# A retention layer with a cosine-gated MLP: another load order at the start, weights released earlier, and the planner's transfer times reset

## The chip, the core and the metric

The kernel runs on one core of one Trainium2 chip. Its engines are TensorE (PE: matmuls; the load of a matmul's stationary operand is shown apart as PEld), VectorE (DVE), ScalarE (ACT), GpSimd (POOL) and SyncE (SP), which here only issues transfers. Each engine runs its own instructions in the order in which they were written; semaphores hold an instruction until what it needs is there. Sixteen DMA engines move the data, fed by queues: `q1` (hardware) carries what SP issues, `q0` (software) what POOL issues. The metric is device microseconds of one execution.

## The reference

Q, K and V have 8 batches, 8 heads, 576 positions and 64 features. The scores are decayed by a power of a constant per head, with no softmax, and the result goes through two matrix products with h cos(h) between them:

```
scores = (q @ k.T) / sqrt(64)
ret    = (scores * gamma_h ** (pos_i - pos_j), zero above the diagonal) @ v     # per batch and head
x      = ret, heads side by side                                                # 4608 x 512
h      = x @ w_in                                                               # 512 -> 2048
out    = (h * cos(h)) @ w_out                                                   # 2048 -> 512, float32
```

The inputs and the output are float32 in memory; matmuls take bf16.

## The kernel before, in words

**Units and blocks.** A unit (b, g) is one batch's 256 positions (g = 0 or 1) or, for g = 2, the last 64 positions of four batches, with all heads. A block is two units: 512 tokens, and there are nine. The first four units in order are (0,0), (1,0), (0,1), (1,1): blocks 0 and 1. For each unit the kernel loads Q, K and V (`load`, L465, issued by SP), scales or casts them to bf16 (`unit`: `qnat`, `natk`, `natv`; the decay is split into a factor on Q and one on V, and `natv` is made by two POOL multiplies), transposes Q and K to `qt`, `kt` (on PE for blocks 0 and 1, `tpe`, L525; by DMA for the rest, `txb`, L540), multiplies K by Q (`scores`), masks on DVE (`pt`, L611), adds up a running state K^T V per batch (`st`, with copies `sba`, `sbb`, `sbr`), and forms the output from masked scores and state (`outputs`), which ACT copies from PSUM to `xt` (L461).

**The MLP.** `mlp1` (L762) multiplies one slice f of 128 hidden features by `win`, over half a block (256 columns) or all of it (512); ACT takes the sine of the result shifted by pi/2 (`cb`, L770) and DVE multiplies it back in (`gt`, L773). `wino2` (L867) is the second matmul in a form with seven products for eight; it needs sums of `gt` (`S`, L828 and L834) and of `wout` (`wsums`, L807), all on DVE. Before the change the blocks 0, 1 and 2 go through `mlp1` in halves, the others whole. Slices go in the order of FORDER: slab 0 of `win` (f 0 to 3), then slabs 2, 1 and 3. A slab of `win` or `wout` is a quarter of the matrix, loaded and cast by a transfer that POOL issues (L742, L746).

**The planner.** None of this order is written out. Each operation becomes a task with an engine, a duration in ns, its readers and writers and, for some, a due time (`prio`). `Graph.run` places tasks one by one at the time at which engine, operands and buffers would be free, by those durations, and the order of the placed tasks becomes the program. For a transfer it takes all transfers as one line: a duration `dma` behind the previous one, and then `tail` until the data may be used. A task with `port=True` is kept from running beside one of the other of DVE and POOL. PSUM has six banks `bk`; a PE task that takes more than two at once may be picked ahead of others to get them (the list `due`, L251). Where the plan leaves a gap on PE, `emit` puts in filler matmuls on a matrix of ones (`warm`, L409). So a changed duration in the planner changes no instruction, only the place of instructions in each engine's line.

**The start before.** SP issues K, Q, V of (0,0), then K, Q, V of (1,0). Slabs 0 and 2 of `win` wait for the K of (1,0), slabs 1 and 3 for its Q. The loads of (0,1) and (1,1) wait for slab 2, the slabs of `wout` for the Q of (1,1), and the loads of (2,0) for slab 2 of `wout`.

Of the kernel before, what the change touches and what calls it, by code (L numbers as in the profile page):

```python
# [11 lines left out]
B, H, S, D = 8, 8, 576, 64  # L12
# [117 lines left out]
class Graph:  # L130


    BACKLOG = 2500
    AHEAD, FETCH = 2000, 6500

    def __init__(self, pools):
        self.tasks, self.wr, self.rd = [], {}, {}
# [70 lines left out]
    def run(self, dma_rate):  # L208
        self.prios()
        free = {e: 0.0 for e in ("pe", "act", "dve", "pool", "sp")}  # L210
# [3 lines left out]
        est, order = {}, []  # L214
# [19 lines left out]
        def pick(e):  # L234
            cand = []
            for t in ready[e]:
                a = slots(t)
                if a is None:
                    continue
                s = max(free[e], est[t], a)  # L240
                if e == "pe" and t.count:
                    k = (seen + t.count - 443) // 256
                    if k >= 0 and 443 + 256 * k > seen and k in asked:
                        s = max(s, asked[k] + self.FETCH - t.dur * (443 + 256 * k - seen) / t.count)
                if t.port:
                    s = max(s, port_free["pool" if e == "dve" else "dve"])
                if t.dma is not None and e != "pool":
                    s = max(s, dma_free - self.BACKLOG)
                cand.append((s, t))
            if e == "pe":  # L250
                due = [t for t in ready[e] if all(any(f is not None and f <= free[e] + 1500 for f in self.pools[b.pool])  # L251
                                                  for b in t.allocs if b.pool != "bk") and self.first(t) and sum(b.pool == "bk" for b in t.allocs) > 2 and est[t] <= free[e] + 1500]
# [12 lines left out]

        n = 0
        while n < len(self.tasks):
# [9 lines left out]
            s, t = best  # L277
            e = t.eng
# [14 lines left out]
            for b in t.allocs:  # L293
                pool = self.pools[b.pool]
# [28 lines left out]
class Kernel:  # L323
# [4 lines left out]
                sbb=(256, BF16), sbr=(256, BF16), xt=(2048, BF16), gt=(NF * TB, BF16), s=(1024, BF16),  # L328
                cb=(TB, BF16), os=(1024, F32), sn=(TB, F32))
    FORDER = [0, 1, 2, 3, 8, 9, 10, 11, 4, 5, 6, 7, 12, 13, 14, 15]  # L330
    SPLIT = 2
    NOXBAR = {0, 1}
    PERIOD, T0, T1 = 28800, 14000, 30000

# [124 lines left out]
    def copy(self, eng, dur, dst, src, r, w, **kw):  # L459
        if eng == "act":  # L460
            return self.one(eng, dur, lambda e: e.activation(dst(), src(), AF.Copy), r=r, w=w, **kw)  # L461
        return self.one(eng, dur, lambda e: e.tensor_copy(dst(), src()), r=r, w=w, port=True, **kw)  # L462


    def load(self, which, u, rows, gate):  # L465

        stg = self.staged[which, u] = Buf("stg" + which)
        src = self.src["qkv".index(which)]
        for i, (p0, n, o, ny, b, r0) in enumerate(rows):
            at, w = (b * H * S + r0) * D, ny * D  # L470
            self.one("sp", 500, lambda e, p0=p0, n=n, o=o, w=w, at=at: e.dma_start(  # L471
                ap(self.at(stg), 1024, p0, n, o, [w, H], [1, w]), bass.AP(src, at, [[w, n], [S * D, H], [1, w]])),
                r=gate, w=[(stg, i)], sem=lambda i=i: f"{which}{stg.slot}_{i}", dma=1830 if ny == 2 else 600, tail=720)
        return stg

    def unit(self, u, fast=False, gate=()):

        rem = u[1] == 2
        t = self.tiles[u] = {}
        for which, nat, dst in (("k", "natk", "kt"), ("q", "qnat", "qt"), ("v", "natv", None)):  # L480
            if rem:
                rows = [(64 * (b % 2), 64, 512 * (b // 2), 1, 4 * u[0] + b, 512) for b in range(4)]
            else:
                rows = [(0, 128, 0, 2, u[0], 256 * u[1])]
            stg = self.load(which, u, rows, gate)
            rs = [(stg, i) for i in range(len(rows))]
            nb = t[nat] = Buf(nat)
            for y in range(2):
                def out(y=y, nb=nb):
                    return ap(self.at(nb), 1024, 0, 128, 512 * y, [256, 2], [64, 4], [1, D])  # L490

                o, w = (512 * y, D) if rem else (D * y, 2 * D)
                hs = [[4, 2], [1, 4]] if which == "v" else [[1, 2], [2, 4]]

                def inp(stg=stg, o=o, hs=[[n * w, c] for n, c in hs]):
                    return ap(self.at(stg), 1024, 0, 128, o, *hs, [1, D])
                if which == "k":
                    eng = ("act", "pool")[y] if fast else "pool"
                    self.copy(eng, {"act": 520, "dve": 610, "pool": 560}[eng], out, inp, rs, [(nb, y)])
                else:  # L500
                    tab, key = (self.WV, "wv") if which == "v" else (self.WQ, "wq")
                    col = 32 if rem else 16 * u[1] + 8 * y
                    eng = "dve" if fast and which == "q" else "pool"
                    self.one(eng, 610 if eng == "dve" else 1000, lambda e, out=out, inp=inp, tab=tab, col=col, hs=hs: e.tensor_tensor(  # L504
                        out(), inp(), ap(tab, 40, 0, 128, col, *hs, [0, D]), ALU.mult),
                        r=rs + [(key,)], w=[(nb, y)], port=True)
# [29 lines left out]
    def txb(self, u):  # L536
        parts = []
        for i, (nat, dst) in enumerate((("natk", "kt"), ("qnat", "qt"))):
            src, dst = self.tiles[u][nat], self.tiles[u][dst]
            parts.append((1300 * (i + 1), lambda e, src=src, dst=dst: e.dma_start_transpose(  # L540
                ap(self.at(dst), 1024, 0, 128, 0, [128, 8], [1, 128]), ap(self.at(src), 1024, 0, 128, 0, [1, 1024])),
                [(src, y) for y in range(2)], [(dst, y) for y in range(2)],
                {"sem": lambda dst=dst: f"t{dst.pool}{dst.slot}"}))
        self.G.add("sp", 2600, parts, dma=4300)

    LANES = [(i, j) for i in range(2) for j in range(2)]

# [101 lines left out]
    def outputs(self, u, prio, late, join=None):  # L649
# [57 lines left out]
        def copies():  # L707
            for s in range(2):
# [3 lines left out]
                else:  # L712
                    dst = lambda s=s: ap(self.at(xt), 2048, 0, 128, 1024 * half + 128 * s, [256, 4], [1, 2], [2, 64])
                    src = lambda s=s: ap(self.at(ob[s]), 512, 0, 128, 0, [128, 4], [64, 2], [1, 64])
                self.copy("act", 590, dst, src, [(ob[s],)], [(xt, half, s)])

        if join is not None:
            join.append((main, cross, reads, writes, copies))
# [21 lines left out]
    def load_w(self, which, s, gate, prio):  # L740
# [4 lines left out]
        else:  # L745
# [64 lines left out]
    def wino2(self, j, base, span):  # L810

        gt = self.gt[j]
        S_ = {(i, q): Buf("s") for i in range(1, 5) for q in range(2)}

        def a(k, h, q):
            return ap(self.at(gt), NF * TB, 0, 128, (8 * k + 4 * q) * TB + 256 * h, [TB, 4], [1, 256])
# [7 lines left out]
        for q in range(2):  # L824
            for i, x, y, r, op in (
                    (1, lambda q=q: a(0, 1, q), lambda q=q: a(1, 1, q), ak(0, 1, q) + ak(1, 1, q), ALU.add),
                    (2, lambda q=q: sv(1, q), lambda q=q: a(0, 0, q), ak(0, 0, q) + [(S_[1, q],)], ALU.subtract)):
                self.one("dve", 610, lambda e, i=i, q=q, x=x, y=y, op=op: e.tensor_tensor(sv(i, q), x(), y(), op),  # L828
                         r=r, w=[(S_[i, q],)], port=True, name=f"S{i}_{j}")
        for q in range(2):  # L830
            for i, x, y, r, op in (
                    (3, lambda q=q: a(0, 0, q), lambda q=q: a(0, 1, q), ak(0, 0, q) + ak(0, 1, q), ALU.subtract),
                    (4, lambda q=q: a(1, 0, q), lambda q=q: sv(2, q), ak(1, 0, q) + [(S_[2, q],)], ALU.subtract)):
                self.one("dve", 610, lambda e, i=i, q=q, x=x, y=y, op=op: e.tensor_tensor(sv(i, q), x(), y(), op),  # L834
                         r=r, w=[(S_[i, q],)], port=True, name=f"S{i}_{j}")
# [71 lines left out]
    def graph(self):  # L907
# [46 lines left out]
        for x in range(4):  # L954
            self.load_w("wout", x, gate, 200 + x)
# [55 lines left out]
```

## Time and profile before

| | us |
|---|---|
| median of 3 runs | 303.77 (302.33 to 304.1) |
| the profiled execution | 302.27 |
| its span in the profile | 300.6 |
| PE busy | 284.7 (95%) |
| DVE busy | 224.1 (75%) |
| ACT busy | 169.2 (56%) |
| POOL busy | 104.2 (35%) |

The profile shows one execution. An engine's busy time is the time in which at least one of its instructions was running; a matmul is counted for about 0.27 us although the next follows after 0.11 us, so a busy PE is not always a PE at its full rate. "Idle before" names what ended a wait, by the semaphore that came last. The granted clock is the share of full speed that the throttle allowed PE.

### The profile page before, as it was taken

To read this page: it belongs to the slowest core of one execution; us is meant where nothing else is said; L and a number is where in the kernel's file an instruction comes from. 1 tells how busy PE (TensorE), PEld (TensorE's weight loads), DVE (VectorE), ACT (ScalarE), POOL (GpSimd) and SP (SyncE) were. 2 spreads that over 40 slices of the span, in tenths; PEclk is the share of its full clock that TensorE was granted. 3 is DMA by queue.
4 is the path that set the end of the run, shared out by engine and by line. 5 is a ranking of instruction groups with operands and counts; after the bars stand their busy time and mean duration, and the time that the engine had idled before them with its cause. 6 is when DMAs were issued, how large, how long until landed. Compare 5 with 4: busy or idle time off the path is not lost.

```text
span 300.6 us, 9042 instructions
## 1 busy us (share of the span) xinstructions
PE 284.7 (95%) x3785; PEld 202.8 (67%) x3785; DVE 224.1 (75%) x390; ACT 169.2 (56%) x315; POOL 104.2 (35%) x125
## 2 busy tenths in 40 slices
PE   7789799999898999999999999999999999999994
PEld 2457577788687876667676767666766676666683
DVE  3667998999994889697959595968687857666721
ACT  5468785468556565645564556465554574545420
POOL 3821970885749204826263515071100000000000
PEclk9999999999999999999999999999999999999999
DMA  7999799999999279996999995782103000300115
GB/s 202 252 206 287 185 180 233 258 240 315 252 274 227 63 186 285 217 226 203 184 301 199 262 218 115 175 218 65 37 1 142 2 2 2 140 0 2 71 72 140
DMA packets 101640, 49.87 MB, mean 166 GB/s; under 512 B 43488, under 2 KB 97248, under 8 KB 101600
## 3 DMA queue, kind: packets, MB, share of 16 engines
q1 hardware_dynamic: 97376, 45.10, 62.8%
q0 software_dynamic: 4224, 4.19, 8.7%
q8 instruction: 30, 0.49, 0.7%
q14 instruction: 10, 0.08, 0.1%
HBM read 36.70 MB, written 9.44 MB: 154 GB/s over the span
## 4 chain that ended last, share of the span: by engine, by line
PE 75%; DMA 13%; POOL 5%; ACT 2%; DVE 2%; issue 1%; SPq 0%; DVEq 0%
PE bk L762 35%; PE bk L867 33%; DMA stgq<-in_q_dram 7%; PE bk L571 6%; DMA wout<-in_moe_w_out_dram 4%; DMA win<-in_moe_w_in_dram 3%; POOL natv L504 2%; PE st L571 1%; POOL qnat L504 1%; ACT xt L461 1%; DVE gt L773 1%; ACT cb L770 0%; POOL wout L746 0%; DVE s L828 0%; SPq L471 0%
## 5 line engine op out<-in xcount | busy, mean ns | idle before, releaser
L770 ACT ACTIVATE cb<-bk,cpi 128x256 bf16<-128x256 f32 (+1 forms) x192 | 108.1, 584 | 82.5 <-PE bk L762 79.2
L762 PE MATMUL bk<-xt,win 128*128 128x256 bf16 (+1 forms) x768 | 143.2, 326 | 2.7 <-issue 1.5
L773 DVE TENSOR_TENSOR gt<-bk,cb 128x256 bf16<-128x256 f32 (+1 forms) x192 | 103.0, 553 | 50.1 <-ACT cb L770 46.5
L762 PEld LDWEIGHTS bk<-xt,win 128*128 128x128 bf16 x768 | 71.9, 98 | 40.6 <-issue 2.7
L504 POOL TENSOR_TENSOR natv<-stgv,wv 128x512 bf16<-128x512 f32 x36 | 40.0, 1134 | 34.6 <-PE bk L571 20.4
L611 DVE TENSOR_TENSOR pt<-bk,tr 128x512 bf16<-128x512 f32 x68 | 42.6, 679 | 2.8 <-PE bk L571 2.8
L504 POOL TENSOR_TENSOR qnat<-stgq,wq 128x512 bf16<-128x512 f32 x32 | 35.1, 1119 | 18.5 <-DMA stgq<-in_q_dram 18.5
L462 POOL CAST natk<-stgk 128x512 bf16<-128x512 f32 x34 | 21.9, 670 | 53.4 <-DMA stgk<-in_k_dram 40.9
L867 PE MATMUL bk<-wout,gt 128*128 128x256 bf16 x288 | 36.7, 273 | 2.4 <-DVE gt L773 1.5
L867 PE MATMUL bk<-tw,s 128*128 128x256 bf16 x288 | 36.9, 273 | 1.0 <-ACT xt L461 1.0
L867 PE MATMUL bk<-wout,s 128*128 128x256 bf16 x288 | 36.4, 273 | 0.0
L867 PEld LDWEIGHTS bk<-tw,s 128*128 128x128 bf16 x288 | 27.8, 98 | 9.7 <-ACT xt L461 1.2
L867 PEld LDWEIGHTS bk<-wout,gt 128*128 128x128 bf16 x288 | 27.6, 98 | 9.4 <-issue 1.8
L867 PEld LDWEIGHTS bk<-wout,s 128*128 128x128 bf16 x288 | 27.8, 98 | 6.5
L461 ACT ACTIVATE sn<-bk 128x512 f32<-128x512 f32 x27 | 16.1, 597 | 17.2 <-PE bk L867 17.2
L879 DVE TENSOR_TENSOR os<-bk,sn 128x512 f32<-128x512 f32 x27 | 18.4, 681 | 9.2 <-PE bk L867 9.2
L461 ACT ACTIVATE xt<-bk 128x512 bf16<-128x512 f32 x36 | 23.7, 728 | 0.5 <-PE bk L571 0.5
L867 PE MATMUL bk<-tw,gt 128*128 128x256 bf16 x144 | 18.5, 273 | 0.0
L867 PEld LDWEIGHTS bk<-tw,gt 128*128 128x128 bf16 x144 | 14.1, 98 | 4.2
L834 DVE TENSOR_TENSOR s<-gt 128x1024 bf16<-128x1024 bf16 x18 | 15.4, 858 | 0.2
L828 DVE TENSOR_TENSOR s<-gt 128x1024 bf16<-128x1024 bf16 x18 | 15.1, 836 | 0.5
L834 DVE TENSOR_TENSOR s<-gt,s 128x1024 bf16<-128x1024 bf16 x18 | 14.7, 815 | 0.2
(56 smaller groups left out, 166.9 us busy)
## 6 DMA issues: line engine op xcount, KB each, us to landing
stgk<-in_k_dram SPq DMA_DIRECT2D x16, 512.0 KB, 6.5
stgq<-in_q_dram SPq DMA_DIRECT2D x16, 512.0 KB, 7.1
stgv<-in_v_dram SPq DMA_DIRECT2D x16, 512.0 KB, 6.7
out_dram<-os SPq DMA_DIRECT2D x16, 512.0 KB, 3.2
win<-in_moe_w_in_dram POOLq DMA_DIRECT2D x4, 512.0 KB, 9.1
wout<-in_moe_w_out_dram POOLq DMA_DIRECT2D x4, 512.0 KB, 10.3
stgk<-in_k_dram SPq DMA_DIRECT2D x8, 128.0 KB, 3.5
stgq<-in_q_dram SPq DMA_DIRECT2D x8, 128.0 KB, 3.3
```

The costliest lines, as they stand in the source:

```text
L461: return self.one(eng, dur, lambda e: e.activation(dst(), src(), AF.Copy), r=r, w=w, **kw)
L462: return self.one(eng, dur, lambda e: e.tensor_copy(dst(), src()), r=r, w=w, port=True, **kw)
L504: self.one(eng, 610 if eng == "dve" else 1000, lambda e, out=out, inp=inp, tab=tab, col=col, hs=hs: e.tensor_tensor(out(), inp(), ap(tab, ...
L571: return lambda e: e.matmul(out(), lhs(), rhs(), start=start, stop=True, skip_group_check=True)
L611: self.one("dve", 610, lambda e, r=r, b=b, pt=pt: e.tensor_tensor(ap(self.at(pt), 1024, 0, 128, 512 * r, [64 * ny * ny, 8 // ny // ny], [1 ...
L762: inst = e.matmul(ap(self.at(bk), 512, 0, 128, 0, [1, n]), ap(self.WIN, 4 * DFF, 0, 128, c * DFF + 128 * f, [1, 128]), ap(self.at(xt), 204 ...
L770: self.one("act", 70 + n, lambda e: e.activation(ap(self.at(cb), TB, 0, 128, 0, [1, n]), ap(self.at(bk), 512, 0, 128, 0, [1, n]), AF.Sin, ...
L773: self.one("dve", 75 + n / 0.96, lambda e: e.tensor_tensor(ap(self.at(gt), NF * TB, 0, 128, f * TB + 256 * h0, [1, n]), ap(self.at(bk), 51 ...
L828: self.one("dve", 610, lambda e, i=i, q=q, x=x, y=y, op=op: e.tensor_tensor(sv(i, q), x(), y(), op), r=r, w=[(S_[i, q],)], port=True, name ...
L834: self.one("dve", 610, lambda e, i=i, q=q, x=x, y=y, op=op: e.tensor_tensor(sv(i, q), x(), y(), op), r=r, w=[(S_[i, q],)], port=True, name ...
L867: inst = e.matmul(ap(self.at(bank), 512, 0, 128, 256 * tt, [1, 256]), l(f, tt), rr(f), start=(first and f == 0 and tt == 0), stop=True, sk ...
L879: self.one("dve", 610, lambda e: e.tensor_tensor(view(h, c), ap(self.at(bank), 512, 0, 128, 0, [256, 2], [1, 256]), ap(self.at(sn[name]), ...
```

## The change

At the start (units built with `fast`) Q is loaded and prepared ahead of K. Slab 0 of `win` waits for the Q of unit (0,0), slab 2 for the Q of (1,0), slabs 1 and 3 for the K of (1,0). `mlp1` of block 0 goes in halves only for slabs 0 and 2, and whole for slabs 1 and 3; block 2 goes whole (SPLIT 1). For three units (SWIFT) one of the two copies to `xt` moves from ACT to DVE. The S sums of block 0 wait for slab 0 of `wout`. In the planner, the time to use of later loads goes from 720 to 1800 ns, the weights' from 2600 + 1500 to 2750 or 3000 + 1900, the DMA transposes' from 4300 to 3000, two POOL durations grow by 20 and 30 ns, DVE copies from PSUM and DVE's multiplies of Q no longer keep POOL away, and the scores of (0,1) may be picked ahead although they take two banks (DUE).

```diff
+    DUE = ("ses/0.1",)
...
-    ... sum(b.pool == "bk" for b in t.allocs) > 2 and est[t] <= free[e] + 1500]
+    ... sum(b.pool == "bk" for b in t.allocs) > 2 - (t.name in self.DUE) and est[t] <= free[e] + 1500]
...
-    SPLIT = 2
+    SPLIT = 1
+    HALVES = (0, 2)
+    SWIFT = ((0, 0), (1, 0), (0, 1))
...
-        return self.one(eng, dur, lambda e: e.tensor_copy(dst(), src()), r=r, w=w, port=True, **kw)
+        return self.one(eng, dur, lambda e: e.tensor_copy(dst(), src()), r=r, w=w, port=eng == "pool", **kw)
...
-                ..., dma=1830 if ny == 2 else 600, tail=720)
+                ..., dma=1840 if ny == 2 else 600, tail=720 if fast else 1800)
...
-        for which, nat, dst in (("k", "natk", "kt"), ("q", "qnat", "qt"), ("v", "natv", None)):
+        todo = [("k", "natk", "kt"), ("q", "qnat", "qt"), ("v", "natv", None)]
+        for which, nat, dst in [todo[i] for i in ((1, 0, 2) if fast else (0, 1, 2))]:
...
-        self.G.add("sp", 2600, parts, dma=4300)
+        self.G.add("sp", 2600, parts, dma=3000)
...
-                self.copy("act", 590, dst, src, [(ob[s],)], [(xt, half, s)])
+                self.copy("dve" if s and u in self.SWIFT else "act", 590, dst, src, [(ob[s],)], [(xt, half, s)])
...
-                 sem=f"{which}{s}", dma=2600, tail=1500, prio=prio)
+                 sem=f"{which}{s}", dma=2750 if which == "win" else 3000, tail=1900, prio=prio)
...
+        late = [("wout", 0, 0)] * (j == 0)
...
-                         r=r, w=[(S_[i, q],)], port=True, name=f"S{i}_{j}")
+                         r=r + late, w=[(S_[i, q],)], port=True, name=f"S{i}_{j}")
...
-        for x, which, pr in ((0, "k", 100), (2, "k", 101), (1, "q", 102), (3, "q", 103)):
-            self.load_w("win", x, [(st[which, (1, 0)], 0)], pr)
+        for x, which, pr in ((0, "q", 100), (2, "q", 101), (1, "k", 102), (3, "k", 103)):
+            self.load_w("win", x, [(st[which, (min(x, 1), 0)], 0)], pr)
...
-        for h in range(2):
-            for i, f in enumerate(self.FORDER):
-                self.mlp1(0, f, (h,), T0 + 435 * (2 * i + h))
+        for i, f in enumerate(self.FORDER):
+            for ses in ((0,), (1,)) if f // 4 in self.HALVES else ((0, 1),):
+                self.mlp1(0, f, ses, T0 + 435 * (2 * i + ses[0]))
```

More of the change, by code (lines that the diff above doesn't have):

```diff
@@ L251, in pick @@
                 due = [t for t in ready[e] if all(any(f is not None and f <= free[e] + 1500 for f in self.pools[b.pool])
-                                                  for b in t.allocs if b.pool != "bk") and self.first(t) and sum(b.pool == "bk" for b in t.allocs) > 2 and est[t] <= free[e] + 1500]
+                                                  for b in t.allocs if b.pool != "bk") and self.first(t) and sum(b.pool == "bk" for b in t.allocs) > 2 - (t.name in self.DUE) and est[t] <= free[e] + 1500]
                 due = [t for t in due if t.prio <= min(x.prio for x in ready[e]) + self.AHEAD]
@@ L461, in copy, with load @@
             return self.one(eng, dur, lambda e: e.activation(dst(), src(), AF.Copy), r=r, w=w, **kw)
-        return self.one(eng, dur, lambda e: e.tensor_copy(dst(), src()), r=r, w=w, port=True, **kw)
-    def load(self, which, u, rows, gate):
+        return self.one(eng, dur, lambda e: e.tensor_copy(dst(), src()), r=r, w=w, port=eng == "pool", **kw)
+    def load(self, which, u, rows, gate, fast):
         stg = self.staged[which, u] = Buf("stg" + which)
@@ L472, in load @@
                 ap(self.at(stg), 1024, p0, n, o, [w, H], [1, w]), bass.AP(src, at, [[w, n], [S * D, H], [1, w]])),
-                r=gate, w=[(stg, i)], sem=lambda i=i: f"{which}{stg.slot}_{i}", dma=1830 if ny == 2 else 600, tail=720)
+                r=gate, w=[(stg, i)], sem=lambda i=i: f"{which}{stg.slot}_{i}", dma=1840 if ny == 2 else 600, tail=720 if fast else 1800)
         return stg
@@ L484, in unit @@
                 rows = [(0, 128, 0, 2, u[0], 256 * u[1])]
-            stg = self.load(which, u, rows, gate)
+            stg = self.load(which, u, rows, gate, fast)
             rs = [(stg, i) for i in range(len(rows))]
@@ L498, in unit @@
                     eng = ("act", "pool")[y] if fast else "pool"
-                    self.copy(eng, {"act": 520, "dve": 610, "pool": 560}[eng], out, inp, rs, [(nb, y)])
+                    self.copy(eng, {"act": 520, "dve": 610, "pool": 580}[eng], out, inp, rs, [(nb, y)])
                 else:
@@ L503, in unit @@
                     eng = "dve" if fast and which == "q" else "pool"
-                    self.one(eng, 610 if eng == "dve" else 1000, lambda e, out=out, inp=inp, tab=tab, col=col, hs=hs: e.tensor_tensor(
+                    self.one(eng, 610 if eng == "dve" else 1030, lambda e, out=out, inp=inp, tab=tab, col=col, hs=hs: e.tensor_tensor(
                         out(), inp(), ap(tab, 40, 0, 128, col, *hs, [0, D]), ALU.mult),
-                        r=rs + [(key,)], w=[(nb, y)], port=True)
+                        r=rs + [(key,)], w=[(nb, y)], port=eng == "pool")
             if dst:
@@ L834, in wino2 @@
                 self.one("dve", 610, lambda e, i=i, q=q, x=x, y=y, op=op: e.tensor_tensor(sv(i, q), x(), y(), op),
-                         r=r, w=[(S_[i, q],)], port=True, name=f"S{i}_{j}")
+                         r=r + late, w=[(S_[i, q],)], port=True, name=f"S{i}_{j}")
         A, Bb, C = Buf("bk"), Buf("bk"), Buf("bk")
```

## The prediction

> **What bounds the kernel now.** I read the page's engine shares first, then the busy time by stage, then the PE timeline of the start and the DMA queues. Busy time by stage (columns: PE, PEld, DVE, ACT, POOL busy us with instruction counts, granted clock, DMA share, GB/s):
>
> ```profile
> 0.00:17.00 17.00, 12.93 (x192) 6.63 (x192) 8.51 (x28) 8.81 (x15) 10.63 (x25) 1.00 0.99 224
> 17.00:28.00 11.00, 9.70 (x143) 7.83 (x144) 7.53 (x19) 8.35 (x20) 0.46 (x1) 1.00 1.21 246
> 28.00:46.00 18.00, 14.95 (x233) 11.55 (x231) 17.39 (x32) 13.73 (x31) 14.27 (x16) 1.00 0.97 196
> 46.00:100.00 54.00, 50.99 (x830) 42.23 (x829) 46.45 (x88) 33.52 (x76) 33.22 (x34) 1.00 1.12 255
> 100.00:283.00 183.00, 182.73 (x2275) 122.87 (x2273) 139.26 (x220) 101.08 (x168) 45.66 (x50) 1.00 0.56 131
> ```
>
> From 100 to 283 us PE idles 0.27 us: nothing is to be won there. The tail (PE ends at 296.4, span 300.6) is the last product and its store, in the same order after the change. So only the first 100 us count. Steady rates: eight 256-wide matmuls take 0.87 us (0.109 each), eight 512-wide 1.73 (0.216), 32 attention matmuls 0.57, eight transposes 0.45. All the work at these rates is 384 x 0.109 + 384 x 0.216 + 1008 x 0.109 + 1920 x 0.0178 + 64 x 0.057 = 272.5 us; PE ends at 296.4, so 23.9 us are lost: 12.8 before 17.0 (only 4.2 us of work is done by then), some 2.2 to 26.8, 4.5 from there to 46, and 4.4 to 100. PE stretches at the start:
>
> ```profile
> 1.12 4.02 PE L409 MATMUL bk<-one 128*128 128x512 bf16 x9 [1.12 <-DVE lg L432]
> ...
> 9.45 0.64 PE L571 MATMUL bk<-qt,kt 64*64 64x128 bf16 x32
> ...
> 16.99 0.61 PE L762 MATMUL bk<-xt,win 128*128 128x256 bf16 x4 [0.17 <-DMA win<-in_moe_w_in_dram]
> ...
> 20.44 2.12 PE L762 MATMUL bk<-xt,win 128*128 128x256 bf16 x18 [1.28 <-issue]
> ...
> 45.70 1.05 PE L867 MATMUL bk<-wout,gt 128*128 128x256 bf16 x8 [0.83 <-DMA wout<-in_moe_w_out_dram]
> ```
>
> The first product waits for `win` slab 0 until 16.99. The 1.28 us at 20.44 stop in the middle of a group of four, where the program has no wait; the page calls it issue.
>
> **Q ahead of K, unit (0,0).** The same six loads in another order: Q lands where K did (about 5.0), K where Q did (6.8). Before, after Q at 6.81 came two DVE multiplies in series (1.29), a transpose, a copy, scores at 9.45. After, the multiplies are done by 6.4 while K flies; K's two casts run beside each other (ACT 0.63, POOL 0.61), then transpose 0.24, copy 0.60: scores at 8.7. The four mask multiplies (0.63 each) end at 11.7 instead of 13.54, since DVE no longer stops among them for the second Q (landed 12.2).
>
> **The first slab's release.** Slab 0 moves from behind unit (1,0)'s K to behind (0,0)'s Q, past two POOL instructions (K's cast and natv): its issue (3.17 us for four, so 0.8) falls into POOL's idle time until 5.06 and costs nothing there. Slab 2 now waits for (1,0)'s Q, slabs 1 and 3 for its K, 1.6 us ahead of (1,0)'s natv. Issue to landing was 5.6 us for slab 0, so 10.6 at the earliest. The price is paid by the loads that the slab now runs among. A slab moves in 2.6 us (11 us for four), a load in 1.8. What two queues do to each other is seen once, when the loads of unit (0,1) were issued at 20.54 against the last slab. From 22 to 23.5 the slabs' queue alone moved; from 24 to 26 both did:
>
> ```profile
> q0 software_dynamic: 305, 0.31, 124.2%
> ```
> ```profile
> q1 hardware_dynamic: 1255, 0.63, 108.7%
> q0 software_dynamic: 28, 0.02, 6.7%
> ```
>
> So bounds for V of (1,0), the last of the six: 16.7 if the slabs queue behind loads already issued (13.4 before plus a slab, plus the tail to landing), 24.6 if all slabs go first, as in the first of these windows. I take 18.6, packets sharing once both queues are fed, since the new loads are in flight before the slabs, unlike at 20.54; both ends stay in the range. [...]
>
> PE then: V of (0,0) lands between 8.9 and 11.1 (its natv starts at 8.76 now; the slab takes up to 2.4 from it), natv takes 2.08 on POOL, outputs end at 13 to 14.5; the transposes of (1,0)'s Q (landing 13.6) stand ahead of the first product, so it starts at 15.3 against 16.99. Sixteen matmuls (1.74), K's transposes and scores run to 18.2; natv of (1,0) is done at 18.6 + 2.08 + 0.3 = 21.0 and slab 2 lands at about 20.5 to 21, so PE stands some 2.5 us; then four products, outputs and 44 products end at 27.6 (26.8 at the near bound). Before, 58 of these 64 were done at 26.8. SP's next loads, those of (0,1), wait for slab 2 as they did (20.5), and move by no more than half a us. Gain 0 to 0.7, **I take 0.3**: the start mostly swaps a wait for the slab for a wait for V.
>
> **Half or full width.** Blocks 0 (half of it) and 2 go to 512 columns: 48 halves become 24 wholes. PE's columns are the same. The rows:
>
> ```profile
> L770 ACT ACTIVATE cb<-bk,cpi 128x512 bf16<-128x512 f32 x96 | 66.1, 689 | 64.2 <-PE bk L762 63.8
> L770 ACT ACTIVATE cb<-bk,cpi 128x256 bf16<-128x256 f32 x96 | 42.0, 480 | 18.3 <-PE bk L762 15.4 <-DVE gt L773 2.8
> ```
> ```profile
> L773 DVE TENSOR_TENSOR gt<-bk,cb 128x512 bf16<-128x512 f32 x96 | 65.5, 688 | 39.2 <-ACT cb L770 38.0 <-PE bk L867 0.5
> ...
> L773 DVE TENSOR_TENSOR gt<-bk,cb 128x256 bf16<-128x256 f32 x96 | 37.4, 419 | 10.9 <-ACT cb L770 8.5 <-PE bk L762 2.0
> ```
>
> ACT saves 48 x 0.480 - 24 x 0.689 = 6.5 us, DVE 48 x 0.419 - 24 x 0.688 = 3.6 and takes three `xt` copies from ACT. No row has that copy on DVE: between 0.42 (its bf16 copy of a bank) and 0.73 (ACT's own); I take 0.68, as its combine of a bank: 2.0. Net DVE -1.6 us, in the stages where it is busy 17.39 of 18 and 46.45 of 54 us.
>
> **The planner's times.** They cost no instruction; they move the order. Between 28 and 46 the sums of block 0 (S, L828/L834), which kept DVE busy then, go behind `wout` slab 0, and products of block 1 come ahead of block 0's second matmul. I walk the new PE order with the rows: after the 64 products, eight full ones, then transposes of (0,1) between full products to 33; scores; 0.5 us for K's cast of (1,1), since POOL works in series from 27 to 43 as before; 0.6 for the masks of (0,1); 40 half products, two `wout` groups: 46.2 with 2.0 us lost against 4.5, of which the 0.83 above is one. **2.5 us.** The added wait for `wout` slab 0 (landed at 41.1) stands on DVE ahead of (1,1)'s masks; DVE reaches it at 43.1, so 2 us of cover; beyond that each us is PE's. From 46 on DVE has 25 gt x 0.43, 8 S x 0.8, 5 tw and 2 wout x 0.7, 3 combines and 4 masks x 0.68 = 26.8 us of queue beside 23.8 us of PE work: PE waits about 2.5 to 3 against 4.4 before. **1.7 us.** Each walk could miss as much as it finds (0 for both) or leave half the losses still more (1 us each way).
>
> **Sum.** 0.3 + 2.5 + 1.7 = 4.5. A walk by hand finds only the waits it looks for; I take four fifths, 3.6 us. The profiled execution took 302.27 (span 300.6 and 1.7 around it), 1.5 under the median 303.77; the new runs may fall on either, so I set out from 303.0: **299.4**.
>
> **Rivals.**
> *Within 1%: nothing but the start's small gain (0 to 2 us, 301 to 303).* For it: DVE is full in 28 to 90 us and stays so; a stop removed on PE returns as a wait for DVE. Against: S moves out of 28 to 46, and ACT and DVE lose instructions. This also covers the case that the new planner times change the order but not the time.
> *Slower: V of (1,0) starves.* If three slabs run unshared from 16 to 24, V lands at 24.6, natv ends at 26.7, the 64 products at 33.0 instead of 27.6: 5.4 late. Later waits swallow 1 us; with the later gains kept the end is near 302, with half of them lost near 306. It decides from V landing past about 22. For it the 22 to 23.5 window, against it the 24 to 26 one.
> *The PE clock.* The nine 512-wide matmuls at 1.12 take 4.02 us, 0.45 each, the three at 6.48 take 0.81: PE runs at half speed until it has been busy. The change issues 24 filler matmuls for 25, in smaller handfuls, and I see 2.5 us of standing at 18 to 21. If the slow rate returned for 5 us, 2.5 us of work would be lost: near 302. The granted clock reads 1.00 in all stages before. [...]
>
> **Chances.** Forecast 0.53; nothing 0.22; V starved 0.18; clock 0.07 (counted as within 1%, apart from 0.02 slower). Faster by over 1% (about what a measurement of this kernel can tell) 0.53, within 1% 0.27, slower 0.20. Range 295 (the near bound for V and a walk that misses nothing, 8 us) to 306 (V starved, half the later gains).
>
> **What would show it.** Scores at 8.7; first product at 15.3; V's natv of (1,0) starting at 18 to 19; PE's lost time 28 to 100 down from 9 to about 5; L770 at 48 half and 120 full instructions; still no idle from 100 on. Wrong if natv of (1,0) starts past 22, if DVE's idle time in 46 to 100 stays but PE's does not shrink, or if PE idles after 100.

## The result, and the profile after

The changed kernel takes **299.25 us** (median of four runs, 298.31 to 300.12) against 303.16 us before (four runs, 302.33 to 304.1): a ratio of 0.9868, 95% interval 0.9829 to 0.9908. The profiled execution took 298.82 us with a span of 297.1; before it was 302.27 and 300.6. The forecast was 299.4. The total agrees, but the terms under it do not, and that is what the experiments are about. Of some kernels below a part of the executions took over 1.5% longer than the fastest, at a lower granted clock (six of ten for the start alone, 308.23 to 310.55 us at a mean clock of 0.986 to 0.993, the other four at 0.998 to 1.0), and the ratios leave these out.

Busy time by stage of the kernel after, in the columns of the table in the prediction (PE, PEld, DVE, ACT, POOL busy us with counts, granted clock, DMA share, GB/s):

```profile
0.00:17.00 17.00, 13.86 (x169) 7.80 (x169) 9.13 (x30) 8.61 (x17) 8.73 (x24) 1.00 1.02 236
17.00:28.00 11.00, 10.67 (x168) 7.64 (x166) 8.98 (x20) 7.81 (x18) 2.81 (x4) 1.00 1.20 249
28.00:46.00 18.00, 17.03 (x269) 11.51 (x268) 13.89 (x25) 13.65 (x27) 12.60 (x15) 1.00 0.98 195
46.00:100.00 54.00, 53.59 (x791) 39.78 (x790) 49.50 (x82) 30.92 (x61) 32.77 (x32) 1.00 1.13 257
100.00:283.00 183.00, 180.55 (x2211) 119.29 (x2210) 139.70 (x212) 100.17 (x164) 49.82 (x52) 1.00 0.59 133
```

PE's visible idle time, row by row against the row of before: 17 to 28 us 0.33 for 1.30, 28 to 46 us 0.97 for 3.05, 46 to 100 us 0.41 for 3.01, and 100 to 283 us **2.45 for 0.27**. The first three give 5.65 us, the last takes 2.18 back. DVE in 28 to 46 is down from 17.39 to 13.89 us.

By the measure of the prediction (stage length less the work done in it at steady rates) the lost time up to 28 us fell from 14.73 to 13.39, in 28 to 46 from 4.38 to 2.59, in 46 to 100 from 4.16 to 0.87, and from 100 to 283 it rose by about 2.6. That is 1.3 + 1.8 + 3.3 - 2.6 = 3.8 us, where the two profiled executions differ by 3.45. A matmul on the edge of a window is counted on both sides, which moves the last figure by some 0.3 us.

PE stretches of the kernel after, start and length in us (those that answer to the ones shown of before):

```profile
9.34 0.95 PE L575 MATMUL bk<-qt,kt 64*64 64x128 bf16 x32 [0.18 <-DVE kt L465]
...
14.83 1.03 PE L766 MATMUL bk<-xt,win 128*128 128x256 bf16 x8
...
21.43 6.70 PE L766 MATMUL bk<-xt,win 128*128 128x256 bf16 x52
...
45.04 1.04 PE L872 MATMUL bk<-wout,gt 128*128 128x256 bf16 x8
```

The first product starts at 14.83 (before 16.99) with no wait for `win`, the 1.28 us stop at 20.44 is gone, and so is the wait for `wout` at 45.70. For a while the loads and the slab did share. In 10.5 to 12.5 us the two queues moved almost as many packets each:

```profile
q0 software_dynamic: 283, 0.29, 83.9%
q1 hardware_dynamic: 280, 0.14, 34.7%
```

In 13 to 15 us they did not: the loads' queue moved 1299 packets and the slabs' queue one, although slab 2 had been issued at 10.71. POOL's multiply of V of (1,0) started at 16.92, as soon as V had landed, and not at 18.6:

```profile
16.92 2.04 POOL L508 TENSOR_TENSOR natv<-stgv,wv 128x512 bf16<-128x512 f32 x2 [0.22 <-DMA stgv<-in_v_dram]
```

Behind 100 us the waits of PE are three kinds, all for DVE (waits view: us in total, times, longest):

```profile
PE bk L872 <- DVE s L833: 1.0, 1, 1.0
PE bk L766 <- DVE pt L615: 0.8, 2, 0.5
PE bk L766 <- DVE gt L777: 0.6, 2, 0.3
```

and the longest falls where DVE's sums take far more than the 0.68 us that they take elsewhere (DVE timeline):

```profile
104.22 1.06 DVE L833 TENSOR_TENSOR s<-s,gt 128x1024 bf16<-128x1024 bf16 x1
105.20 1.53 DVE L833 TENSOR_TENSOR s<-gt 128x1024 bf16<-128x1024 bf16 x1
106.65 1.09 DVE L839 TENSOR_TENSOR s<-gt 128x1024 bf16<-128x1024 bf16 x1
107.66 1.09 DVE L833 TENSOR_TENSOR s<-s,gt 128x1024 bf16<-128x1024 bf16 x1
```

I had passed over this slowness in the profile before, where the sums' group means are 725 to 858 ns. Sorted by whether POOL computes at the same time, the sums in the kernel before take 0.685 us each when POOL is idle or issuing transfers (52 of 72) and 1.13 us on average, up to 1.53, when it computes (20 of 72). After: 0.686 (48) and 1.10 (24). The multiplies `gt` (128x512) take 0.684 either way, so it is not DVE as a whole that slows down.

The longest stop of PE behind 46 us in the kernel before came from this. DVE, POOL and PE of that kernel:

```profile
72.94 1.53 DVE L834 TENSOR_TENSOR s<-gt 128x1024 bf16<-128x1024 bf16 x1
74.39 1.52 DVE L834 TENSOR_TENSOR s<-gt,s 128x1024 bf16<-128x1024 bf16 x1
```
```profile
71.42 2.50 POOL L504 TENSOR_TENSOR qnat<-stgq,wq 128x512 bf16<-128x512 f32 x2 [3.35 <-DMA stgq<-in_q_dram]
73.89 2.94 POOL L504 TENSOR_TENSOR natv<-stgv,wv 128x512 bf16<-128x512 f32 x2
```
```profile
76.40 1.03 PE L867 MATMUL bk<-wout,gt 128*128 128x256 bf16 x8 [1.54 <-DVE gt L773]
```

Two sums of block 1 took 1.5 us each beside POOL's multiplies, the `gt` queued behind them came late, and PE stood 1.54 of the 3.01 us that it idled in 46 to 100. In 28 to 46 the share is smaller: of 3.05 us PE's waits name DVE for 1.1 (0.53 of them a `gt` behind two sums of 1.5 us), a slab of `wout` for 0.8 and POOL for 0.7.

### The profile page after: what moved, and what is told of

The parts are those of the page before. It is cut to its first block, busy times and chain, and to the rows that moved or that the text cites. A ratio compares the mean times of both kernels' runs of the same rounds, so it can differ in the third digit from the quotient of the medians.

```text
span 297.1 us, 8758 instructions
## 1 busy us (share of the span) xinstructions
PE 285.6 (96%) x3688; PEld 194.6 (66%) x3688; DVE 223.8 (75%) x369; ACT 163.0 (55%) x288; POOL 106.7 (36%) x125
## 4 chain that ended last, share of the span: by engine, by line
PE 75%; DVE 16%; ACT 4%; issue 3%; DMA 1%; DVEq 0%
PE bk L766 38%; PE bk L872 27%; PE bk L575 6%; DVE pt L615 4%; DVE s L833 4%; DVE gt L777 4%; ACT cb L774 3%; DVE s L839 2%; DMA stgq<-in_q_dram 1%; PE st L575 1%; PE bk L529 1%; DVE tw L811 1%; DVE os L884 1%; ACT qt L464 0%; ACT kt L464 0%
## 5 line engine op out<-in xcount | busy, mean ns | idle before, releaser
L774 ACT ACTIVATE cb<-bk,cpi 128x512 bf16<-128x512 f32 (+1 forms) x168 | 103.3, 629 | 81.1 <-PE bk L766 79.3
L766 PE MATMUL bk<-xt,win 128*128 128x512 bf16 (+1 forms) x672 | 141.7, 349 | 2.2 <-DVE pt L615 1.1
L777 DVE TENSOR_TENSOR gt<-bk,cb 128x512 bf16<-128x512 f32 (+1 forms) x168 | 99.9, 610 | 47.2 <-ACT cb L774 46.3
L766 PEld LDWEIGHTS bk<-xt,win 128*128 128x128 bf16 x672 | 63.3, 98 | 45.8 <-DVE pt L615 2.0
L465 POOL CAST natk<-stgk 128x512 bf16<-128x512 f32 x34 | 24.1, 733 | 44.5 <-DMA stgk<-in_k_dram 23.9
L464 ACT ACTIVATE xt<-bk 128x512 bf16<-128x512 f32 x33 | 21.7, 725 | 0.5 <-PE bk L575 0.5
L839 DVE TENSOR_TENSOR s<-gt,s 128x1024 bf16<-128x1024 bf16 x18 | 15.6, 873 | 0.2
L833 DVE TENSOR_TENSOR s<-gt 128x1024 bf16<-128x1024 bf16 x18 | 14.6, 816 | 0.4
L833 DVE TENSOR_TENSOR s<-s,gt 128x1024 bf16<-128x1024 bf16 x18 | 14.6, 814 | 0.4
```

Of the source, the lines that this page charges most:

```text
L766: inst = e.matmul(ap(self.at(bk), 512, 0, 128, 0, [1, n]), ap(self.WIN, 4 * DFF, 0, 128, c * DFF + 128 * f, [1, 128]), ap(self.at(xt), 204 ...
L774: self.one("act", 70 + n, lambda e: e.activation(ap(self.at(cb), TB, 0, 128, 0, [1, n]), ap(self.at(bk), 512, 0, 128, 0, [1, n]), AF.Sin, ...
L777: self.one("dve", 75 + n / 0.96, lambda e: e.tensor_tensor(ap(self.at(gt), NF * TB, 0, 128, f * TB + 256 * h0, [1, n]), ap(self.at(bk), 51 ...
```

## The experiments

Ratios are against the kernel before, run beside each. "Wide DVE operations before 46" counts the sums and `wout` sums, all on 128x1024 tiles, that start before 46 us; "standing" is their time beyond what they take alone: 0.685 us for one, and 0.6 for each further one where the timeline joins several in a row.

| kernel | ratio (95%) | wide DVE operations before 46 | standing before 46, us |
|---|---|---|---|
| before | 1 | 7 | 3.1 |
| after | 0.9868 (0.9829 to 0.9908) | 1 | 0.0 |
| after, slab 0 late | 0.9902 (0.9871 to 0.9933) | 1 | 0.0 |
| after, old planner times | 0.9913 (0.9873 to 0.9953) | 1 | 0.0 |
| after, old widths | 0.9840 (0.9796 to 0.9883) | 1 | 0.0 |
| after, copies on ACT | 0.9892 (0.9853 to 0.9932) | 1 | 0.0 |
| after, block 2 in halves | 0.9857 (0.9809 to 0.9905) | 1 | 0.0 |
| after, sums free | 1.0018 (0.9997 to 1.0039) | 7 | 3.3 |
| after, sums free, copy on ACT | 1.0047 (1.0013 to 1.0081) | 8 | 4.1 |
| after, sums free, POOL fills | 0.9811 (0.9765 to 0.9858) | 9 | 1.0 |
| before + start | 1.0003 (0.9977 to 1.0030) | 8 | 2.1 |
| before + planner times | 1.0026 (0.9990 to 1.0063) | 9 | 2.3 |
| before + the sums' wait | 1.0118 (1.0080 to 1.0155) | 5 | 0.9 |
| before + start + the sums' wait | 1.0042 (1.0007 to 1.0076) | 5 | 0.9 |

Of the kernels that do all the work, those whose sums start behind 46 us gain 0.9 to 1.6%, and those with sums before 46 us gain nothing or lose. No part of the change that I ran by itself gains. The edit that lets the scores of (0,1) be picked ahead (DUE) was neither undone nor run by itself.

### The changed kernel, one part undone at a time

**Without the sums' wait.**

```diff
-        late = [("wout", 0, 0)] * (j == 0)
+        late = []
```

> The changed kernel, but the S sums of block 0 do not wait for slab 0 of wout. Theory A (the wait keeps the sums out of 28 to 46, worth 1.3 us there): DVE busy 28 to 46 back to 17 of 18 us, PE idle there up by 1 to 2 us; the sums no longer meet POOL at 104 to 108, so up to 1 us of the waits behind 100 goes: time 299.3 to 300.5. Rival B (the wait costs more behind 100 us than it brings before 46): time 297.5 to 298.7.

It took 303.99 us: this one wait is worth all that the change gains (0.015 between the ratios, about 4.6 us), and neither theory had that. By stage it lost 7.5 us in 28 to 46 (the changed kernel 2.6) and 2.9 in 46 to 100 (0.9), and won 1.1 back behind 100. DVE, POOL and PE of this kernel tell why:

```profile
37.36 3.95 DVE L839 TENSOR_TENSOR s<-gt 128x1024 bf16<-128x1024 bf16 x1
41.23 0.68 DVE L777 TENSOR_TENSOR gt<-bk,cb 128x512 bf16<-128x512 f32 x1
41.83 0.71 DVE L465 CAST xt<-bk 128x512 bf16<-128x512 f32 x1
```
```profile
37.12 2.09 POOL L508 TENSOR_TENSOR qnat<-stgq,wq 128x512 bf16<-128x512 f32 x2
39.12 0.64 POOL L465 CAST natk<-stgk 128x512 bf16<-128x512 f32 x1
39.69 2.51 POOL L508 TENSOR_TENSOR natv<-stgv,wv 128x512 bf16<-128x512 f32 x2
```
```profile
42.69 4.43 PE L766 MATMUL bk<-xt,win 128*128 128x256 bf16 x20 [3.61 <-DVE xt L465]
```

One sum, of a kind that takes 0.68 us when POOL does not compute, ran from 37.36 to 41.31, past two multiplies and a cast of POOL and into its next two multiplies; of POOL's work in that time those two took longer (2.51 us, where two take 2.04 alone). The copy to `xt` stands behind it in DVE's line, and PE stood 3.61 us for it. The stop had a second price. Granted clock of this kernel by windows (PE busy, clock, DMA share, GB/s):

```profile
39.00:41.00 2.00, 0.09 (x2) 1.00 1.07 159
41.00:43.00 2.00, 0.31 (x2) 0.50 1.20 196
43.00:45.00 2.00, 2.00 (x12) 0.50 1.24 207
45.00:47.00 2.00, 2.00 (x11) 0.50 1.24 206
47.00:49.00 2.00, 2.00 (x20) 0.80 1.04 257
```

The clock fell to half 1.9 us into the stop and came back at about 47.8, 5 us after PE had work again; the 20 matmuls behind the stop took 4.43 us, where 20 took 2.36 at a clock of 1.00 (the kernel before, at 23.54).

**Without the wait, and the copy of (0,1) on ACT.**

```diff
-    SWIFT = ((0, 0), (1, 0), (0, 1))
+    SWIFT = ((0, 0), (1, 0))
...
-        late = [("wout", 0, 0)] * (j == 0)
+        late = []
```

> The changed kernel without the sums' wait, as in the run that took 304.0, but the copy to xt of unit (0,1) stays on ACT. Theory A (the 3.6 us stop and the halved clock behind it came from that copy standing behind the sums in DVE's order; the wait is needed only because the copy went to DVE): no stop over 1.5 us in 38 to 46, granted clock 1.00, time 299.5 to 300.8. Rival B (the sums hold PE wherever they stand in 37 to 44, by the products' banks that DVE empties late): stops of 2 us or more in all in 38 to 48, time 301.5 to 303.5.

Theory A falls: ratio 1.0047. The same sum stood 3.82 us, and PE waited for the `gt` behind it instead of the copy:

```profile
37.30 3.82 DVE L839 TENSOR_TENSOR s<-gt 128x1024 bf16<-128x1024 bf16 x1
```
```profile
41.78 1.48 PE L766 MATMUL bk<-xt,win 128*128 128x256 bf16 x12 [1.53 <-DVE gt L777]
```

PE stood 1.53 us there, and the clock held in that stage, so the copy on ACT did help: 28 to 46 lost 5.1 us, where it lost 7.5 without the wait and 2.6 in the changed kernel. Of rival B, the stops of 2 us in 38 to 48 came (0.60 and 1.53), but its time did not. Part of the time has another cause: the profile has a stop of 2.50 us up to 102.4 that is named issue, which I can't explain, and behind it the clock was at half from about 102.8 to 106.2.

**Without the wait, and POOL filling instead of reading.** The order on every engine is that of the kernel without the wait; only six POOL instructions differ, all of unit (1,1): two casts of K, two multiplies of Q and two of V become fills with zero. This kernel leaves out Q, K and V of that unit.

```diff
-                    self.copy(eng, {"act": 520, "dve": 610, "pool": 580}[eng], out, inp, rs, [(nb, y)])
+                    if u == (1, 1):
+                        self.one(eng, 580, lambda e, out=out: e.memset(out(), 0.0), r=rs, w=[(nb, y)], port=True)
+                    else:
+                        self.copy(eng, {"act": 520, "dve": 610, "pool": 580}[eng], out, inp, rs, [(nb, y)])
...
-                    self.one(eng, ..., lambda e, ...: e.tensor_tensor(
+                    self.one(eng, ..., lambda e, ...: e.memset(out(), 0.0) if u == (1, 1) else e.tensor_tensor(
...
-        late = [("wout", 0, 0)] * (j == 0)
+        late = []
```

> The run without the sums' wait (304.0 us) again, with every engine's order unchanged, but POOL's five operations on unit (1,1) (K casts, Q and V multiplies) are fills with zero that read no tile; this leaves out Q, K and V of that unit. Theory A (a sum of DVE that reads two tiles from SBUF stands still while POOL's multiplies and casts run; this made one sum of 0.68 us last 3.95 us at 37.4, the copy to xt behind it late, PE stand 3.6 us and its clock fall to half): the sum takes 0.7 us, PE's stop at 39 is under 0.8 us, the granted clock stays 1.00, time 298.5 to 300.5. Rival B (the copy is late because of the number and place of the sums on DVE, whatever POOL does): the stop stays at 2 us or more, time 302.5 to 304.5.

Theory A holds: 298.0 us, 6 less than with the reading instructions and half a us below A's range. The clock stayed at 1.00 in 28 to 46, though not at the start (see the last section). DVE and POOL of this kernel:

```profile
38.41 0.68 DVE L842 TENSOR_TENSOR s<-gt 128x1024 bf16<-128x1024 bf16 x1
39.01 0.69 DVE L780 TENSOR_TENSOR gt<-bk,cb 128x512 bf16<-128x512 f32 x1
39.61 0.72 DVE L465 CAST xt<-bk 128x512 bf16<-128x512 f32 x1
```
```profile
37.91 0.57 POOL L504 MEMSET natk<- 128x512 bf16 x1
38.38 1.04 POOL L511 MEMSET natv<- 128x512 bf16 x2
```

The sum ran inside the fills' time and took 0.68, and PE's stop for the copy was 0.33 us. 28 to 46 lost 2.58 us, as in the changed kernel (2.59). So it is not POOL's being busy as such that holds the sum: it took 0.68 us beside the fills, which read no tile, and 3.95 beside the casts and multiplies, which do. The fills are also shorter than the multiplies (0.5 for 1.03 us), so part of the 6 us may be POOL's earlier end.

**Slab 0 late again.**

```diff
-            self.load_w("win", x, [(st[which, (min(x, 1), 0)], 0)], pr)
+            self.load_w("win", x, [(st[which, (1, 0)], 0)], pr)
```

> The changed kernel, but slab 0 of win is released by the Q of unit (1,0), as the other early slab is, instead of the Q of (0,0). Theory A (the trace of the changed kernel is read rightly: 1.3 us of its gain come from the earlier slab, and V of (1,0) pays nothing for it): first product back at about 17, the natv of (1,0) no earlier than 16.9, lost PE time to 28 us up by 1.0 to 1.5, time 300.0 to 301.0. Rival B (the slab only swaps one wait for another, as the prediction's walk had it; the gain is the order that the planner found behind it): time within 0.5 us of the changed kernel, about 299.3. Rival C (any replanning shifts the time by a us or more): the difference appears at 28 to 283 us, not before 28.

301.13 us, first product at 16.97. The `natv` of (1,0), which A wanted no earlier than 16.9, started at 14.07:

```profile
14.07 2.04 POOL L508 TENSOR_TENSOR natv<-stgv,wv 128x512 bf16<-128x512 f32 x2 [0.33 <-DMA stgv<-in_v_dram]
```

So V does pay for the earlier slab, 2.85 us. By 28 us this kernel had lost 13.45 us, as much as the changed kernel (13.39): up to there the earlier slab swaps a wait for the slab for a wait for V, as rival B has it. It fell behind in 28 to 46 (4.01 lost for 2.59), the sign of C and not that of A. The intervals of the two ratios overlap: the earlier slab's worth lies between nothing and 2 us, and is not settled better.

**Old planner times.**

```diff
-                r=gate, w=[(stg, i)], ..., dma=1840 if ny == 2 else 600, tail=720 if fast else 1800)
+                r=gate, w=[(stg, i)], ..., dma=1830 if ny == 2 else 600, tail=720)
...
-        self.G.add("sp", 2600, parts, dma=3000)
+        self.G.add("sp", 2600, parts, dma=4300)
...
-                 sem=f"{which}{s}", dma=2750 if which == "win" else 3000, tail=1900, prio=prio)
+                 sem=f"{which}{s}", dma=2600, tail=1500, prio=prio)
```

(The two POOL durations and the rule on which DVE work keeps POOL away went back too.)

> The changed kernel with the planner's old transfer times and its old rule on which DVE work keeps POOL away; loads, widths and the sums' wait stay as changed. Theory A (the planner's times carry the gain of 28 to 46 us and part of 46 to 100): lost PE time there rises by 2 us or more, and the waits behind 100 us (2.45 us) shrink as the order there goes back, time 300.5 to 302. Rival B (the widths and the earlier slab carry the gain, the times only reshuffle): time 298.5 to 299.8.

300.43 us. Its profile lost 3.15 in 28 to 46 and 3.17 in 46 to 100 (after: 2.59 and 0.87), and PE's waits behind 100 us shrank to 1.19, as A said, with the time just under A's range. By the ratios (0.9913 for 0.9868) the times are worth about a us, but the intervals overlap.

**Old widths.**

```diff
-    SPLIT = 1
-    HALVES = (0, 2)
+    SPLIT = 2
+    HALVES = (0, 1, 2, 3)
```

> The changed kernel with block 0 and block 2 in halves again, as before. Theory A (the instructions that ACT and DVE are spared buy the gain of 46 to 100): PE idle in 46 to 100 rises by 2 to 3 us, time 301 to 302 if the waits behind 100 us stay, 299 if they go away with the halves. Rival B (DVE's order and not its load decides): time within 0.7 us of 299.3, PE idle in 46 to 100 still under 1 us.

298.63 us, rival B. PE idle in 46 to 100 is 0.97 us (A wanted 2.4 or more), and behind 100 it fell to 0.96. The wider slices buy nothing here.

**All copies on ACT.**

```diff
-    SWIFT = ((0, 0), (1, 0), (0, 1))
+    SWIFT = ()
```

> The changed kernel with all copies to xt on ACT, as before; the sums' wait stays. Theory A (ACT was in the way at the start and at 38 us: the three copies on DVE are worth something): lost PE time to 46 us up by 0.5 to 1.2, time 299.8 to 300.6. Rival B (DVE is the fuller engine, so copies on ACT are better or as good): 298.3 to 299.4.

300.59 us, inside A's range at its upper end; lost time to 46 us 16.87 for 15.98. Its interval overlaps with that of the changed kernel.

**Block 2 in halves.**

```diff
-    SPLIT = 1
+    SPLIT = 2
```

> The changed kernel with block 2 in halves as before (block 0 keeps its new widths). Theory A (block 2 in whole slices causes the waits behind 100 us: its 512-wide products and the slowed sums at 104 to 108 keep DVE full; the run with both blocks in halves took 298.6): PE idle behind 100 us under 1 us, 46 to 100 as in the changed kernel, time 297.5 to 298.8, the fastest yet. Rival B (the waits come from the order that the planner happens on): time within 0.5 us of 299.3 or above.

299.53 us. The sign of A came, without its time: PE idle behind 100 us fell from 2.45 to 1.02, but in 46 to 100 it rose from 0.41 to 0.89. The time is B's. This and the old widths are the best candidates, and neither can be told from the changed kernel.

### The kernel before, with one or two parts alone

**The start alone** (Q ahead of K, slab 0 released by the first Q).

```diff
+        todo = [("k", "natk", "kt"), ("q", "qnat", "qt"), ("v", "natv", None)]
+        for which, nat, dst in [todo[i] for i in ((1, 0, 2) if fast else (0, 1, 2))]:
...
+        for x, which, pr in ((0, "q", 100), (2, "q", 101), (1, "k", 102), (3, "k", 103)):
+            self.load_w("win", x, [(st[which, (min(x, 1), 0)], 0)], pr)
```

> The kernel before with only the start changed: Q ahead of K in the first two units, slab 0 of win released by the first Q. Theory A (the start is worth 1.3 us whatever follows): first product at about 14.8, lost PE time to 28 us down by 1.0 to 1.5, time 301.5 to 302.3. Rival B (DVE, busy 17.4 of 18 us in 28 to 46, takes it back, since the sums still stand there): lost time to 46 us as in the kernel before, time 302.8 to 303.8.

Ratio 1.0003, rival B. The first product started at 14.64 and 1.14 us were won by 17 us; 0.5 was left at 28, and by 60 us it had lost 0.9 more than the kernel before. Eight wide operations ran before 46, and PE waited 1.26 us for a mask behind one of them. But 28 to 46 lost no more than in the kernel before (4.33 for 4.38); the loss came in 46 to 60, where the profile has a stop of 1.80 us named issue. So that the sums took the gain back, as B has it, is not shown.

**The planner's times alone.** The edit of the old planner times, the other way round, in the kernel before.

> The kernel before with only the planner's times changed (later loads, weights, transposes, the two POOL durations, and which DVE work keeps POOL away). Theory A (from the run with the old times in the changed kernel, which was 1.2 us slower: the times are worth about a us by themselves): 301.7 to 302.7, with less lost at 28 to 80. Rival B (without the sums' wait the better times only pull the sums and copies to other places: no gain or a loss): 303 to 304.5.

Ratio 1.0026, rival B. Nine wide operations before 46 us, one of them of 2.21 us at 39.1, and 5.74 us lost in 28 to 46 for 4.38. The longest stop there, 1.37 us up to 45.11, is named issue, and its cause is open.

**The wait alone.**

```diff
+        late = [("wout", 0, 0)] * (j == 0)
...
-                         r=r, w=[(S_[i, q],)], port=True, name=f"S{i}_{j}")
+                         r=r + late, w=[(S_[i, q],)], port=True, name=f"S{i}_{j}")
```

> The kernel before with only the wait of block 0's sums for slab 0 of wout added. Theory A (the wait is the part of the change that pays: it takes 1.1 to 1.5 us of slow sums and their place in DVE's line out of 28 to 46): lost PE time of 28 to 46 down from 4.4 to about 2.5, time 300.8 to 302.2. Rival B (before the change PE found other work there, and the wait only protects the orders with a faster start): within 0.8 us of the kernel before, 302.5 to 304.

306.33 us: slower by 1.2%, so both theories were wrong. The 28 to 46 stage did improve (3.54 lost for 4.38), but 46 to 60 lost 3.79 for 1.03. Released at 41, the sums and the `wout` sums were spread over 41 to 60 us, and the last of them met POOL's next series:

```profile
54.28 1.53 DVE L835 TENSOR_TENSOR s<-gt 128x1024 bf16<-128x1024 bf16 x1
55.74 1.53 DVE L807 TENSOR_TENSOR wout<-wout 128x1024 bf16<-128x1024 bf16 x1
57.19 2.97 DVE L835 TENSOR_TENSOR s<-gt,s 128x1024 bf16<-128x1024 bf16 x2
```
```profile
54.01 2.71 POOL L504 TENSOR_TENSOR qnat<-stgq,wq 128x512 bf16<-128x512 f32 x2 [0.20 <-DMA stgq<-in_q_dram]
56.68 2.93 POOL L504 TENSOR_TENSOR natv<-stgv,wv 128x512 bf16<-128x512 f32 x2
```
```profile
60.64 1.03 PE L762 MATMUL bk<-xt,win 128*128 128x256 bf16 x8 [3.00 <-DVE gt L773]
```

Both engines pay: four wide operations took 5.9 us where four take 2.5 alone, POOL's four multiplies 5.6 where four take 4.1, and PE stood 3.00 us for the `gt` queued behind.

**The start and the wait.** Both edits above together.

> The kernel before with the new start (Q ahead of K, the earlier slab) and the wait of block 0's sums, nothing else. Alone the new start gave no time (ratio 1.000): it gained 1.1 us by 17 us and lost it by 60 us. Theory A (with the sums out of the way the start's gain survives): 300.0 to 301.3, of the 4 us all but what the planner's times and the copies on DVE add. Rival B (the start's gain needs the planner's times or the widths): 302 to 303.5.

Ratio 1.0042, past rival B. The start held (13.96 lost at 28 us for 14.73); 46 to 100 lost 5.76 for 4.16, with a stop of 1.82 us at 59.4 for a POOL multiply of V. The wait needs company: the changed kernel with either the old planner times or the old widths still has its sums behind 46 us; with the start and the wait alone, where times, widths and copies are all old, they begin at 40.7.

## Why the prediction was right, and where it was not

**What bounds the kernel.** The first 100 us, as said; but "PE idle 0.27 us: nothing is to be won there" left out that something can be lost: 2.2 us of idle time came back behind 100, which the prediction itself had named as a sign against it. The sums at 104 to 108 stand there while POOL multiplies and casts without a pause from 101.7 to 110.7. Why the order puts them there is not settled; block 2 in halves took most of that idle time away and put half a us elsewhere.

**Q ahead of K.** Scores were forecast for 8.7 and ran at 9.34 in the profiled execution, but at 8.87 in the kernel with block 2 in halves and at 8.71 in that with POOL fills, whose starts have the same loads. Most of the difference is PE's rate: after, two 512-wide matmuls at 6.82 took 1.06 us, in the other kernel 0.60 at 6.81.

```profile
6.82 1.06 PE L412 MATMUL bk<-one 128*128 128x512 bf16 x2
```
```profile
6.81 0.60 PE L412 MATMUL bk<-one 128*128 128x512 bf16 x2
...
8.87 0.64 PE L575 MATMUL bk<-qt,kt 64*64 64x128 bf16 x32 [0.39 <-DVE kt L465]
```

So the step was right. When the slow rate of the start ends was not the same in these executions: in the kernel with POOL fills two such matmuls took 0.59 us at 6.65, and its granted clock reads 1.00 in 6 to 10 us, as that of the changed kernel does. Up to 8 us PE had been busy for 6.2 us in the changed kernel and for 5.7 in that one, so "until it has been busy" does not give the time.

**The slab's release, 0.3 us.** By 28 us 1.3 us were won, but hardly by the slab: with slab 0 late the changed kernel had won as much by then, with all copies on ACT 0.7 less, and the start alone won 0.5 (one profile each). So 0.3 for the start was about right, and "mostly swaps a wait" too. A term under it was wrong, V of (1,0) at 18.6. Six loads were under way, the slab began to move only at about 9, slab 2 not before 15, and V had landed by 16.9, next to the bound of 16.7 that I had written down. The sharing of packets behind the 18.6 was seen in 10.5 to 12.5 us (280 and 283) and not in 13 to 15 (1299 and one). The first product at 14.83 answers to 15.3.

**Half or full width.** Sized rightly (48 half and 120 full `cb`; the `xt` copy took 0.73 us for my 0.68) and without effect: the old widths cost nothing.

**The planner's times, 2.5 and 1.7.** This is the step that failed, although its sum, 4.2, is near the 5.1 lost less in 28 to 100. I wrote that the sums "kept DVE busy then" and go behind `wout` slab 0, but priced them as DVE work of 0.7 to 0.8 us each and gave the gain to the planner's times and the walk. The runs put it on the wait: without it the new order is 4.6 us slower. That is its worth in the new order, and not a share of what was lost before: there DVE was named for 1.1 us of PE's waits in 28 to 46 and for 1.5 in 46 to 100, and the wait alone made that kernel slower. And the sums' cost is not their work but their standing beside POOL's casts and multiplies, up to 3.95 us for one, 3.1 us in all before 46 in the kernel before; DVE's 17.39 of 18 us were partly standing. This fits both results: the wait pays where it puts the sums behind POOL's series, and loses 1.2% where it puts them into the next one. The cover of 2 us that I gave the wait never mattered.

**Sum.** 4.5 was expected before the cut to four fifths, and 6.4 was won by 100 us; the cut took 0.9, the idle time behind 100 took 2.6. That the total came out within 0.2 us is luck: gains by 100 us that I had put too low met a loss that I had ruled out.

**Rivals.** V did not starve. "DVE is full and a stop comes back as a wait for it" is what happened in the changed kernel without the sums' wait, and a planner whose times change the order but not the time is the run of the times alone (1.0026). The clock did not fall behind 17 us in the changed kernel (1.00 in every stage), but the rival was a real one: without the sums' wait it read 0.50 from 41.0 to about 47.8.

## What to carry to other kernels

Before moving work, sort one operation's durations by what runs beside it: a group mean of 0.84 us hid 0.68 alone and up to 1.53 beside POOL, and a reordering made one of 3.95. A planner's constraint that looks like a cost can be what keeps two engines apart, and its worth depends on the rest of the order: here the same wait was worth 4.6 us in one order and cost 3.6 in another, so undo parts from the new kernel as well as adding them to the old one.

## What the runs showed of the hardware

- A DVE sum of two bf16 tiles took 0.68 us beside a POOL fill (the kernel with POOL fills), 0.685 and 0.686 on average where POOL was idle or issued transfers (the kernels before and after), and 1.13 and 1.10 on average beside POOL's casts and multiplies, up to 1.53 in these two kernels and 3.95 without the sums' wait. DVE's multiplies `gt`, with one operand in PSUM, took 0.684 either way.
- In the kernel without the sums' wait PE's granted clock fell to 0.50 at 41.0 us, 1.9 us into a stop of 3.61, and was back at about 47.8, after 5 us of work. In the run with POOL fills it fell at about 11.6, behind a stop of only 0.94 us at the start, and came back at about 15:

```profile
11.50:12.00 0.50, 0.28 (x10) 0.61 1.15 209
12.00:13.00 1.00, 1.00 (x40) 0.50 1.16 258
...
15.00:16.00 1.00, 1.00 (x12) 0.99 1.25 243
```

- In the changed kernel, while a load and a slab were both under way, the hardware and the software queue moved 280 and 283 packets in 10.5 to 12.5 us. In two other windows they moved nothing like as many each: in 13 to 15 us the hardware queue moved 1299 and the software queue one, though a slab had been issued at 10.71; and the loads of (0,1), issued from 19.41 on while slabs were moving, got nothing in 20 to 22 us, where the software queue moved 414. The first load of all, issued at 0.81, had packets moving by 2.3 us. No run here tells why.
